# Five exp buffers, nine V buffers, and a reordered end of each group of eight heads in a fused attention and MLP kernel

## The chip, the cores and the metric

The kernel runs on one core of one Trainium2 chip. The metric is the device time of one execution in microseconds (us). The core has a matrix engine (PE, with its weight loads PEld), a vector engine (DVE), an activation engine (ACT), a general engine (POOL) and DMA queues; the queue used here is SyncE's (SP). Each engine runs its own list of instructions in order, and semaphores hold an instruction back until what it needs on another engine is done.

## The reference

Attention over 4 batches and 12 heads, 448 tokens, head size 64, with capped scores, and then a two-layer MLP with the activation h·cos(h). All of it is fp32.

```python
scores = scale * np.matmul(q, k.transpose(0, 1, 3, 2))       # q, k, v: 4 x 12 x 448 x 64
scores = cap * np.tanh(scores / cap)
attn = np.exp(scores - max); attn = attn / (sum(attn) + 1e-09)
x = np.matmul(attn, v)                                       # becomes 1792 x 768
h = x @ w_in                                                 # w_in 768 x 2048
out = (h * np.cos(h)) @ w_out                                # w_out 2048 x 768
```

## The kernel before, in words

**Attention.** The 48 heads are worked through in 6 groups `n` of eight (2 batches by 4 heads). A group has 7 chunks `c` of 64 keys, and a chunk has two score tiles (`a` = 0, 1), so there are 84 score tiles `j` and 42 steps `i`, two tiles to a step. For a step PE makes two score tiles (`scores`, L303, each in one of two PSUM slots of the name `pair`), ACT takes the tanh of each (`tanh`, L321) into one SBUF buffer `t` and the exp of both at once (`exp`, L325). PE then multiplies the exps by V (`values`, L387, halves `e` = 0, 1, summed over the seven chunks in two PSUM buffers `acc`), and DVE adds the exps of six chunks up (`add`, L371, L375). At the end of a group two blocks of matmuls by ones (`sums`, L401) give the denominators in a third `pair` tile `z`: one block reads the last chunk's exps, the other DVE's sum. DVE transposes `z` (`norm_sums`, L412), takes the reciprocal (L419), spreads it (L425), multiplies both `acc` by it into `x0` and `x1` (`norm_scale`, L429), and splits each into a high part (`norm_high`, L434) and a low part (`norm_low`, L437), which are the MLP's input.

**Order.** All of this is called from one list: `at(step, time, call)` gives a call the place 3.4·step + time, the list is sorted, and each engine's instructions stand in that order. The step at whose places a group's denominators are made is called the boundary here (`ends`); it comes when the next group's scores are already under way. Weights are turned from fp64 words to pairs of fp32 parts in between (`Weights`; `DECODE` gives the steps): ACT takes a magnitude (L197), DVE does the rest, the last piece's low part being L230 for the first three pieces.

**Buffers.** A tile of a pool can be written when all readers of the tile that was in its place are done. `t` has 4 buffers, and step 0 uses `x0` and `x1` in place of one. V has 14 places of one chunk. `pair` has two slots in PSUM; `z` takes one of them.

**MLP.** 8 groups of two 128-wide units, 4 blocks of tokens each, 32 steps. For a unit PE makes h (`hidden`, L162), ACT and DVE make h·cos(h) in six operations (`turns` L579, `whole_turns` L582, `reduce` L587 and L588, `cosine` L591, `gate` L594) and split it (`high` L597 on ACT, `low` L600 on DVE); PE multiplies by w_out a step later (L628). Step 0's two units start inside attention: `layers.begin` makes their h in `pair` slots, and `layers.first` takes the first unit up to its gate in the buffer `second`. The MLP's own PSUM tiles (`single`, `rest`) lie where attention's two `acc` were, and its SBUF pools where attention's buffers were.

Of the kernel before, what the change touches and what calls it, by code (L numbers as in the profile page):

```python
# [34 lines left out]
DIRECT = 1  # L35
STEP = 3.4
# [219 lines left out]
class Heads:  # L256


    def __init__(self, ctx, tc, banks, qk, v, capt, inv, xh, xl, bounded):
        nc = tc.nc  # L260
        self.nc, self.qk_in, self.v_in, self.capt, self.inv = nc, qk, v, capt, inv
        if bounded:
            self.inv, self.capt = in_register(nc, inv, "inv"), in_register(nc, capt, "cap")
        self.cap_column = capt
        self.xh, self.xl, self.bounded = xh, xl, bounded
        cp = ctx.enter_context(tc.tile_pool(name="a_const", bufs=1))
        self.ld = ctx.enter_context(tc.tile_pool(name="a_ld", bufs=8 if bounded else 4))
# [8 lines left out]
        self.qk, self.v, self.ps, self.ts, self.half, self.left = {}, {}, {}, {}, {}, {}  # L276
        self.sum, self.acc, self.x, self.z, self.r, self.s = {}, {}, {}, {}, {}, {}
# [34 lines left out]
    def tanh(self, j):  # L312
        i, k = divmod(j, 2)
        if k == 0:
            if i or not self.bounded:
                t = self.ts[i] = self.tp.tile([128, 2, 2, S], F32, name="t", tag="t")
                self.half[i] = [t[:, 0], t[:, 1]]
            else:
                self.half[i] = [self.np.tile([128, 2, S], F32, name=f"x{e}", tag=f"x{e}") for e in range(2)]
            self.left[i] = 2  # L320
        self.nc.scalar.activation(self.half[i][k], self.ps.pop(j)[:, :, 0:S], AF.Tanh, scale=self.inv)  # L321

    def exp(self, i):
        for t in [self.ts[i]] if i else self.half[i]:
            self.nc.scalar.activation(t, t, AF.Exp, scale=self.capt)  # L325

    def t(self, n, a, c):
        j = WHERE[n, a, c]
        return self.half[j // 2][j % 2]

    def used(self, n, c):
        for a in range(2):
            i = WHERE[n, a, c] // 2
            self.left[i] -= 1
            if not self.left[i]:
                self.ts.pop(i, None)
                del self.half[i]
# [115 lines left out]
def attention(ctx, tc, banks, busy, second, qk, v, capt, inv, xh, xl, wts, layers):  # L453
# [24 lines left out]
    for n in range(NO):  # L478
        begin = NC * n
        for c in range(NC):  # L480
            at(begin - 2 * NC + 4 + c if n > 1 else n - 1, 0.3 + 0.1 * c, a.load_v, n, c)
# [3 lines left out]
        for c in range(NC):  # L485
# [8 lines left out]
            if 0 < c < NC - 1:  # L494
                at(i, 0.15, a.add, n, c)
            if c:
                at(i + lag, 0.75 if c == NC - 1 else 2.6 if i == 3 else 0.18, a.used, n, c)
            if c == 1:
                at(i + lag, 2.61 if i == 3 else 0.19, a.used, n, 0)
        for m, (part, args) in enumerate([("sums", ()), ("inverse", ()), ("spread", ()), ("scale", (0,)), ("scale", (1,))]):  # L500
            at(i, 1.0 + 0.1 * m, getattr(a, "norm_" + part), n, *args)
# [14 lines left out]
    at(ND, 1.7, layers.first, second)  # L516
    at(ND + 1, 0.9, layers.begin, 1)
# [130 lines left out]
class Layers:  # L648
    def __init__(self, tc, banks, wts, xh, xl, angles, out):
        self.tc, self.nc, self.banks, self.wts, self.xh, self.xl, self.out = tc, tc.nc, banks, wts, xh, xl, out  # L650
        self.angles, self.half_pi, self.quarter = angles, angles[:, 0:1], angles[:, 1:2]
        self.begun = []
# [13 lines left out]
    def first(self, space):  # L666
# [3 lines left out]
        unit.gone = ("turns", "whole_turns", "reduce", "cosine", "gate")  # L670
        for part in unit.gone:
            getattr(unit, part)()

    def open(self, ctx):
# [13 lines left out]
    def step(self, step, prev, older):  # L688
# [23 lines left out]
        if step == 0:  # L712
            units[1].turns()
            units[1].gone = ("turns",)
# [87 lines left out]
```

## Time and profile before

| what | value |
|---|---|
| median of 3 runs | 630.28 us (629.02 to 630.75) |
| profiled execution | 629.2 us, span 627.4 us |
| PE busy | 612.8 us (98%) |
| DVE busy | 485.7 us (77%) |
| ACT busy | 306.3 us (49%) |
| chain that ended last | PE 90%, ACT 6%, DVE 3% |

The span is what the trace covers of the execution; 1.8 us lie around it. The busy shares are means over two very different stages: attention fills the first quarter, the MLP the rest. The page's slices show PE busy in all, and ACT at 90% or more until the ninth of forty.

### The profile page before, as it was taken

The page shows a single profiled execution, that of the slowest core. Times are in us where ns is not written, and L with a number is a line of the kernel's source. Part 1 is how long each engine was busy: PE and PEld are TensorE (multiplying, and loading weights), DVE is VectorE, ACT ScalarE, POOL GpSimd, SP SyncE. Part 2 cuts the span into 40 slices and gives each one's busy share as a digit, 9 for nine tenths or more (in the row PEclk, how much of TensorE's full clock was granted, in tenths as well). Part 3 has the DMA queues.
Part 4 walks back from the last instruction along what each step waited for, and adds up shares of the span by engine and source line. Part 5 has one row for each costly group of instructions (what it writes and reads, how often), then busy time and mean ns, then how long its engine had stood idle before and what let it go on. Part 6 is the DMA issues. An engine that isn't in the chain of part 4 may idle for free.

```text
span 627.4 us, 11992 instructions
## 1 busy us (share of the span) xinstructions
PE 612.8 (98%) x5206; PEld 472.0 (75%) x5207; DVE 485.7 (77%) x643; ACT 306.3 (49%) x384; POOL 55.3 (9%) x36
## 2 busy tenths in 40 slices
PE   8989999999889999999999999999999999999996
PEld 2333333334779898989989898989899898989895
DVE  1587998886878887888886788888887878887574
ACT  6999999998134343334333333433343333334220
POOL 0000000000111111112011111111111211111000
PEclk9999999999899999999999999999999999999999
DMA  7753445101011111211111111112111111110224
GB/s 222 237 183 122 127 161 165 58 3 52 0 52 50 51 53 52 98 50 52 51 50 51 51 51 51 51 51 86 58 60 50 52 51 50 51 51 1 102 75 182
DMA packets 22783, 48.06 MB, mean 77 GB/s; under 512 B 2497, under 2 KB 9921, under 8 KB 22721
## 3 DMA queue, kind: packets, MB, share of 16 engines
q1 hardware_dynamic: 22576, 47.00, 22.5%
q8 instruction: 43, 0.70, 0.4%
q10 hardware_dynamic: 144, 0.20, 0.1%
q14 instruction: 20, 0.16, 0.1%
HBM read 41.68 MB, written 5.51 MB: 75 GB/s over the span
## 4 chain that ended last, share of the span: by engine, by line
PE 90%; ACT 6%; DVE 3%; issue 0%; DMA 0%; DVEq 0%; ACTq 0%
PE single L162 34%; PE pair L628 25%; PE rest L628 12%; PE pair L303 8%; PE acc L387 7%; ACT t L321 3%; ACT t L325 2%; PE pair L401 1%; PE pair L162 1%; PE idle L63 1%; DVE xl L437 1%; PE acc L63 0%; PE single L628 0%; DVE x L429 0%; DVE gl L600 0%
## 5 line engine op out<-in xcount | busy, mean ns | idle before, releaser
L591 ACT ACTIVATE y<-y,angles 128x384 f32<-128x384 f32 (+1 forms) x63 | 42.3, 672 | 122.9 <-DVE y L588 122.9
L321 ACT ACTIVATE t<-pair 128x896 f32<-128x896 f32 x82 | 72.3, 939 | 4.6 <-PE pair L303 4.5
L387 PE MATMUL acc<-t,v 64*32 64x448 f32 x1312 | 72.9, 536 | 0.0
L303 PE MATMUL pair<-qk 64*32 64x448 f32 x1232 | 70.0, 540 | 2.5 <-ACT t L321 2.0
L325 ACT ACTIVATE t<-t 128x1792 f32<-128x1792 f32 x41 | 70.7, 1728 | 0.0
L641 DVE TENSOR_TENSOR acc<-pair,acc 128x1024 f32<-128x1024 f32 (+1 forms) x56 | 60.8, 1086 | 9.1 <-PE pair L628 8.8
L579 ACT ACTIVATE v<-single,angles 128x384 f32<-128x384 f32 (+1 forms) x62 | 39.2, 632 | 53.0 <-PE single L162 52.8
L597 ACT CAST gh<-y 128x384 fp32r<-128x384 f32 (+1 forms) x63 | 35.8, 569 | 51.1 <-DVE y L594 51.1
L197 ACT ACTIVATE u<-w 128x768 f32<-128x768 f32 x32 | 29.0, 907 | 54.8 <-POOL wo2l L230 10.1
L303 PEld LDWEIGHTS pair<-qk 64*32 64x32 f32 x1232 | 20.8, 106 | 43.9 <-ACT t L321 20.2
L600 DVE TENSOR_TENSOR gl<-y,gh 128x384 fp32r<-128x384 f32 (+1 forms) x63 | 51.9, 823 | 2.5 <-ACT gh L597 2.5
L387 PEld LDWEIGHTS acc<-t,v 64*32 64x32 f32 x1312 | 26.2, 107 | 34.9 <-issue 33.0
L582 DVE TENSOR_SCALAR v<-v 128x384 f32<-128x384 f32 (+1 forms) x63 | 24.5, 388 | 35.2 <-ACT v L579 35.2
L371 DVE TENSOR_TENSOR sum<-sum,t 128x1792 f32<-128x1792 f32 x20 | 40.5, 2025 | 9.8 <-ACT t L325 9.8
L212 DVE TENSOR_SCALAR u<-u 128x768 f32<-128x768 f32 x32 | 17.8, 555 | 32.3 <-ACT u L197 32.2
L588 DVE SCALAR_TENSOR_TENSOR y<-v,y 128x384 f32<-128x384 f32 (+1 forms) x63 | 39.3, 624 | 2.2
L594 DVE TENSOR_TENSOR y<-single,y 128x384 f32<-128x384 f32 (+1 forms) x62 | 38.4, 619 | 3.1 <-ACT y L591 3.1
L587 DVE SCALAR_TENSOR_TENSOR y<-v,single 128x384 f32<-128x384 f32 (+1 forms) x62 | 38.3, 618 | 2.1
L162 PE MATMUL single<-xh,wi0h 128*128 128x384 f32 (+1 forms) x90 | 33.1, 368 | 1.9 <-DVE x L429 1.9
L628 PE MATMUL pair<-gh,wo0l 128*128 128x512 f32 (+1 forms) x96 | 34.9, 363 | 0.0
L628 PE MATMUL pair<-gl,wo0h 128*128 128x512 f32 (+1 forms) x96 | 34.8, 363 | 0.0
L628 PE MATMUL pair<-gh,wo0h 128*128 128x512 f32 (+1 forms) x96 | 34.8, 363 | 0.0
(158 smaller groups left out, 1468.7 us busy)
## 6 DMA issues: line engine op xcount, KB each, us to landing
w<-in_w_in_dram SPq DMA_DIRECT2D x32, 384.0 KB, 3.6
w<-in_w_out_dram SPq DMA_DIRECT2D x32, 384.0 KB, 3.6
qk<-in_qk_dram SPq DMA_DIRECT2D x20, 448.0 KB, 4.4
v<-in_v_dram SPq DMA_DIRECT2D x42, 128.0 KB, 3.5
out_dram<-acc SPq DMA_DIRECT2D x6, 512.0 KB, 2.8
out_dram<-acc SPq DMA_DIRECT2D x5, 384.0 KB, 2.4
qk<-in_qk_dram SPq DMA_DIRECT2D x2, 288.0 KB, 2.9
qk<-in_qk_dram SPq DMA_DIRECT2D x2, 160.0 KB, 3.7
```

The source lines that it names most:

```text
L162: nc.tensor.matmul(h[:, 0:n], lhsT=w[:, ks], rhs=x[:, k, toks], start=(k == 0 and i == 0), stop=(k == KC - 1 and i == 2))
L303: self.nc.tensor.matmul(ps[o:o + 32, h, 0:S], lhsT=x[mine, k:k + 32], rhs=x[mine, Q], start=True, stop=True, tile_position=(64 * h, o))
L321: self.nc.scalar.activation(self.half[i][k], self.ps.pop(j)[:, :, 0:S], AF.Tanh, scale=self.inv)
L325: self.nc.scalar.activation(t, t, AF.Exp, scale=self.capt)
L371: self.nc.vector.tensor_add(out, old, self.ts[NC * n + c])
L387: self.nc.tensor.matmul(self.acc[n, e][o, r], lhsT=self.v[n, c][rows, d], rhs=self.t(n, a, c)[rows, h], start=c == 0, stop=c == NC - 1, ti ...
L579: m.nc.scalar.activation(self.v, self.h, AF.Identity, bias=m.quarter, scale=1.0 / (2.0 * math.pi))
L588: m.nc.vector.scalar_tensor_tensor(self.y, self.v, -TWO_PI_LO, self.y, op0=ALU.mult, op1=ALU.add)
L591: self.m.nc.scalar.activation(self.y, self.y, AF.Sin, bias=self.m.half_pi)
L600: self.m.nc.vector.tensor_sub(self.result(1), self.y, self.result(0))
L628: m.nc.tensor.matmul((y[e] if self.last(i) else y[:, e])[:, 0:n], lhsT=w[:, c], rhs=x[:, j, 0:n], start=(j == 0 and k == 0), stop=(j == GF ...
L641: m.nc.vector.tensor_add(acc, y[:, e, 0:n], acc)
```

## The change

What the diff does, in its parts:

- `t` gets 5 buffers, and step 0 uses one of them like every other step, so its exp is one instruction over both tiles. V gets 9 places; its loads are spread over the steps.
- In the first group the values of chunks 1 to 5 all stand behind the two score tiles of their step (time 2.5).
- At a boundary the two `sums` blocks move from before the boundary's first score tile to between its two score tiles, the second half of the last chunk's values goes behind one further score tile, and the two `norm_scale` follow it.
- In the last group `sums` stands ahead of chunk 5's values. `norm_sums` stands ahead of the first unit's gate, and the previous group's low parts ahead of that unit's work.
- A new `begin_rest` writes out step 0 of the MLP: the two units' operations and the last group's high and low parts are interleaved by hand. The low part of `wo1` goes to DVE (it was on POOL). The weights that the MLP adds get an SBUF pool of their own.

The core of the diff:

```diff
-        self.tp = ctx.enter_context(tc.tile_pool(name="a_t", bufs=4 if bounded else NC))
+        self.tp = ctx.enter_context(tc.tile_pool(name="a_t", bufs=5 if bounded else NC))
-        self.v[n, c] = self.ld.tile([128, 256], F32, name="v", tag="v", bufs=2 * NC if self.bounded else NC)
+        self.v[n, c] = self.ld.tile([128, 256], F32, name="v", tag="v", bufs=NV if self.bounded else NC)
...
-            at(begin - 2 * NC + 4 + c if n > 1 else n - 1, 0.3 + 0.1 * c, a.load_v, n, c)
+            at(max(begin + c - NV + 5, n - 1), 0.3 + 0.1 * c, a.load_v, n, c)
...
+        for c in range(NC - 1):
             i = max(WHERE[n, p, c] for p in range(2)) // 2 + 2
-            lag = 1 if c < NC - 1 and 0 < n and (n, c) not in ((NO - 1, NC - 3), (NO - 1, NC - 2)) else 0
-            if c == NC - 1:
-                at(i, 0.15, a.sums, n, c)
-                at(i, 0.16, a.sums, n, None)
+            step = i + (0 < n and not (last and c == NC - 3))
+            time = (2.5, 2.51) if n == 0 and c else (0.1, 2.0) if n == 0 else (0.17, 0.18) if last and c == NC - 2 else (0.1, 0.1)
             for e in range(2):
-                time = (0.5, 0.7) if c == NC - 1 else (0.1, 2.0) if i == 3 and c == 0 else (2.5, 2.51) if i == 3 else (0.1, 0.1)
-                at(i + lag, time[e], a.values, n, c, e)
+                at(step, time[e], a.values, n, c, e)
...
+        b = begin + NC + 1
+        at(b, 0.15 if last else 0.3, a.sums, n, NC - 1)
+        at(b, 0.16 if last else 0.3, a.sums, n, None)
+        at(b, 0.5, a.values, n, NC - 1, 0)
+        at(b + 1, 1.7, a.values, n, NC - 1, 1)
+        at(b + 1, 1.75, a.used, n, NC - 1)
+        at(b, 1.0, a.norm_sums, n)
+        at(b, 1.1, a.norm_inverse, n)
+        at(b, 1.2, a.norm_spread, n)
         for e in range(2):
-            at(i + 2, 0.5, a.norm_high, n, e)
-            at(i + NC if n < NO - 1 else i + 2, 0.9, a.norm_low, n, e)
+            at(b + 1, 1.8 + 0.1 * e, a.norm_scale, n, e)
+            if not last:
+                at(b + 2, 0.5, a.norm_high, n, e)
+                at(b + NC - (n == NO - 2), 0.9, a.norm_low, n, e)
...
-    at(ND, 1.7, layers.first, second)
-    at(ND + 1, 0.9, layers.begin, 1)
+    at(ND, 1.7, layers.first, second, ("turns", "whole_turns", "reduce", "cosine"))
+    at(ND + 1, 1.05, layers.first, second, ("gate",))
+    at(ND + 2, 1.9, layers.begin, 1)
+    layers.late = [(getattr(a, f"norm_{part}"), NO - 1, e) for part in ("high", "low") for e in range(2)]
...
+    def begin_rest(self):
...
+        first.high()
+        first.low()
+        second.turns()
+        self.wts.high(*self.done)
+        late(0)
+        late(1)
+        second.whole_turns()
+        second.reduce()
+        second.cosine()
+        self.wts.low(*self.done, self.nc.vector)
+        second.gate()
+        second.high()
+        late(2)
+        second.low()
+        late(3)
...
+        wp = ctx.enter_context(self.tc.tile_pool(name="m_w", bufs=1))
         accp = ctx.enter_context(self.tc.tile_pool(name="m_acc", bufs=1))
-        self.wts.open_in(accp, (2, 3))
-        self.wts.open_in(accp, (1, 2), "wo")
+        self.wts.open_in(wp, (2, 3))
+        self.wts.open_in(wp, (1, 2), "wo")
...
         if step == 0:
-            units[1].turns()
-            units[1].gone = ("turns",)
+            self.begin_rest()
+            self.done = piece
+            return cur
```

PE at the boundary of the second group. `qk` rows are score tiles, `t,v` rows values, `t,one` and `sum,one` the two sums; eight matmuls are one block, 16 are two. Before:

```order
L387 MATMUL acc<-t,v 32x448 x16
L401 MATMUL pair<-t,one 32x448 x8
L401 MATMUL pair<-sum,one 32x448 x8
L303 MATMUL pair<-qk 32x448 x8
L387 MATMUL acc<-t,v 32x448 x8
L303 MATMUL pair<-qk 32x448 x8
L387 MATMUL acc<-t,v 32x448 x8
L303 MATMUL pair<-qk 32x448 x16
```

and now:

```order
L382 MATMUL acc<-t,v 32x448 x16
L304 MATMUL pair<-qk 32x448 x8
L396 MATMUL pair<-t,one 32x448 x8
L396 MATMUL pair<-sum,one 32x448 x8
L382 MATMUL acc<-t,v 32x448 x8
L304 MATMUL pair<-qk 32x448 x16
L382 MATMUL acc<-t,v 32x448 x8
L304 MATMUL pair<-qk 32x448 x8
```

One score tile has passed the sums, and one more has passed the second half of the values.

PE where attention ends and the MLP's step 0 begins (`xl,wi0h` is the last of the first unit's 18 matmuls, `xh,wi1h` the first of the second unit's). Before:

```order
L162 MATMUL pair<-xl,wi0h 128x512
L387 MATMUL acc<-t,v 32x448 x16
L401 MATMUL pair<-t,one 32x448 x8
L401 MATMUL pair<-sum,one 32x448 x8
L387 MATMUL acc<-t,v 32x448 x16
L162 MATMUL pair<-xh,wi1h 128x512
```

and now:

```order
L163 MATMUL pair<-xl,wi0h 128x512
L396 MATMUL pair<-t,one 32x448 x8
L396 MATMUL pair<-sum,one 32x448 x8
L382 MATMUL acc<-t,v 32x448 x32
L163 MATMUL pair<-xh,wi1h 128x512
```

The sums have passed two blocks of values; what PE does in all between the two units is the same.

DVE at the same place (`second` and `gl<-second` are the first unit's, `v` and `y` the second unit's; `x_1892` and `x_1894` are the fifth group's, the other `x` the sixth's). Before:

```order
L594 TENSOR_TENSOR second<-pair,second 128x512
L437 TENSOR_TENSOR xl<-x_1892,xh 128x896
L437 TENSOR_TENSOR xl<-x_1894,xh 128x896
L412 STREAM_TRANSPOSE s<-pair 128x896
L419 RECIPROCAL r<-s 128x28
L425 STREAM_TRANSPOSE s<-r 128x896
L429 TENSOR_TENSOR x_2185<-acc,s 128x896
L429 TENSOR_TENSOR x_2187<-acc,s 128x896
L434 CAST xh<-x_2185 128x896
L434 CAST xh<-x_2187 128x896
L437 TENSOR_TENSOR xl<-x_2185,xh 128x896
L437 TENSOR_TENSOR xl<-x_2187,xh 128x896
```

and now:

```order
L407 STREAM_TRANSPOSE s<-pair 128x896
L596 TENSOR_TENSOR second<-pair,second 128x512
L414 RECIPROCAL r<-s 128x28
L420 STREAM_TRANSPOSE s<-r 128x896
L424 TENSOR_TENSOR x_2164<-acc,s 128x896
L424 TENSOR_TENSOR x_2166<-acc,s 128x896
L602 TENSOR_TENSOR gl<-second,gh 128x512
L429 CAST xh<-x_2164 128x896
L429 CAST xh<-x_2166 128x896
L584 TENSOR_SCALAR v<-v 128x512
L589 SCALAR_TENSOR_TENSOR y<-v,pair 128x512
L590 SCALAR_TENSOR_TENSOR y<-v,y 128x512
```

The fifth group's low parts stand ahead of the first unit's work now, the transposition ahead of the gate, and the sixth group's low parts behind the second unit's gate.

## Rows read from the trace of the kernel before

**Rows 1.** Windows: span, then us busy (instructions) of PE, PEld, DVE, ACT, POOL; clock, DMA.
```profile
59.20:82.40 23.20, 22.75 (x496) 9.10 (x486) 20.41 (x18) 22.61 (x22) 0.00 (x0) 1.00 0.48 155
164.40:167.90 3.50, 3.48 (x12) 3.48 (x13) 3.04 (x4) 0.37 (x1) 0.00 (x0) 0.54 0.00 0
183.00:300.00 117.00, 117.00 (x585) 105.34 (x584) 96.25 (x141) 45.01 (x68) 17.23 (x9) 1.00 0.18 61
```

**Rows 2.** Timeline, first group on ACT: start, us, engine, line, operation, [idle before].
```profile
20.50 1.75 ACT L325 ACTIVATE t<-t 128x1792 f32<-128x1792 f32 x1
23.06 1.73 ACT L321 ACTIVATE t<-pair 128x896 f32<-128x896 f32 x2 [0.81 <-PE pair L303]
```

**Rows 3.** Waits between 12 and 149 us: who waited for whom, us, times, longest.
```profile
ACT t L321 <- PE pair L303: 3.8, 11, 0.8
```

**Rows 4.** Timeline of the second group's boundary, PE, ACT and DVE.
```profile
57.65 1.80 ACT L321 ACTIVATE t<-pair 128x896 f32<-128x896 f32 x2
...
58.69 0.99 PE L401 MATMUL pair<-t,one 64*32 64x448 f32 x16
...
59.24 1.79 ACT L325 ACTIVATE t<-t 128x1792 f32<-128x1792 f32 x1
...
60.21 0.96 PE L303 MATMUL pair<-qk 64*32 64x448 f32 x16
...
60.53 1.12 DVE L412 STREAM_TRANSPOSE s<-pair 128x896 f32<-128x896 f32 x1 [1.37 <-PE pair L401]
...
61.28 0.92 ACT L321 ACTIVATE t<-pair 128x896 f32<-128x896 f32 x1 [0.25 <-PE pair L303]
...
63.26 2.09 DVE L429 TENSOR_TENSOR x<-acc,s 128x896 f32<-128x896 f32 x2
...
64.64 0.99 PE L303 MATMUL pair<-qk 64*32 64x448 f32 x16 [0.45 <-ACT t L321]
...
66.92 1.71 PE L303 MATMUL pair<-qk 64*32 64x448 f32 x32
...
68.14 1.72 ACT L321 ACTIVATE t<-pair 128x896 f32<-128x896 f32 x2
```

**Rows 5.** Timeline after the fourth group's boundary: a weight piece's low part, the next magnitude.
```profile
117.61 0.95 DVE L230 TENSOR_TENSOR wo0l<-u,wo0h 128x768 fp32r<-128x768 f32 x1
118.70 0.98 ACT L197 ACTIVATE u<-w 128x768 f32<-128x768 f32 x1
```

**Rows 6.** Timeline from the last sums to the MLP's first products.
```profile
154.28 0.43 DVE L582 TENSOR_SCALAR second<-second 128x512 f32<-128x512 f32 x1 [2.81 <-ACT second L579]
...
156.94 0.69 DVE L594 TENSOR_TENSOR second<-pair,second 128x512 f32<-128x512 f32 x1 [0.79 <-ACT second L591]
...
158.12 0.50 PE L162 MATMUL pair<-xh,wi1h 128*128 128x512 f32 x1
...
162.28 2.09 DVE L429 TENSOR_TENSOR x<-acc,s 128x896 f32<-128x896 f32 x2
...
164.42 0.47 PE L162 MATMUL single<-xh,wi0h 128*128 128x384 f32 x1 [1.93 <-DVE x L429]
...
167.53 0.83 ACT L448 CAST wo1h<-u 128x768 fp32r<-128x768 f32 x1 [4.26 <-DVE xl L437]
...
168.92 1.92 DVE L600 TENSOR_TENSOR gl<-second,gh 128x512 fp32r<-128x512 f32 x1 [1.48 <-ACT gh L597]
170.76 0.42 DVE L582 TENSOR_SCALAR v<-v 128x512 f32<-128x512 f32 x1
...
174.13 0.62 ACT L597 CAST gh<-y 128x512 fp32r<-128x512 f32 x1 [0.76 <-DVE y L594]
...
175.53 0.50 PE L628 MATMUL pair<-gl,wo1h 128*128 128x512 f32 x1
```

**Rows 7.** Chain that ended last, in order of time: start, us, engine and line.
```profile
197.30 6.24 PE single L162 x36
```

**Rows 8.** DMA issues of the page: count, KB each, us from issue to landing.
```profile
v<-in_v_dram SPq DMA_DIRECT2D x42, 128.0 KB, 3.5
```

More of the change, by code (lines that the diff above doesn't have):

```diff
@@ L275, in __init__ @@
             make_identity(nc, self.ident)
-        self.qk, self.v, self.ps, self.ts, self.half, self.left = {}, {}, {}, {}, {}, {}
+        self.qk, self.v, self.ps, self.ts, self.left = {}, {}, {}, {}, {}
         self.sum, self.acc, self.x, self.z, self.r, self.s = {}, {}, {}, {}, {}, {}
@@ L314, in tanh @@
         if k == 0:
[L315 to L319, printed above, removed]
+            self.ts[i] = self.tp.tile([128, 2, 2, S], F32, name="t", tag="t")
             self.left[i] = 2
-        self.nc.scalar.activation(self.half[i][k], self.ps.pop(j)[:, :, 0:S], AF.Tanh, scale=self.inv)
+        self.nc.scalar.activation(self.ts[i][:, k], self.ps.pop(j)[:, :, 0:S], AF.Tanh, scale=self.inv)
     def exp(self, i):
-        for t in [self.ts[i]] if i else self.half[i]:
-            self.nc.scalar.activation(t, t, AF.Exp, scale=self.capt)
+        self.nc.scalar.activation(self.ts[i], self.ts[i], AF.Exp, scale=self.capt)
     def t(self, n, a, c):
         j = WHERE[n, a, c]
-        return self.half[j // 2][j % 2]
+        return self.ts[j // 2][:, j % 2]
     def used(self, n, c):
@@ L335, in used @@
             if not self.left[i]:
-                self.ts.pop(i, None)
-                del self.half[i]
+                del self.ts[i]
     def exp_general(self, n):
@@ L478, in attention @@
     for n in range(NO):
-        begin = NC * n
+        begin, last = NC * n, n == NO - 1
         for c in range(NC):
-            at(begin - 2 * NC + 4 + c if n > 1 else n - 1, 0.3 + 0.1 * c, a.load_v, n, c)
+            at(max(begin + c - NV + 5, n - 1), 0.3 + 0.1 * c, a.load_v, n, c)
         for p in range(4):
@@ L484, in attention @@
                 at(begin - NC + (-1, 2, 3, 4)[p] if n > 1 else -0.5, 0.8, a.load, n, p // 2, p % 2)
-        for c in range(NC):
+        for c in range(NC - 1):
             i = max(WHERE[n, p, c] for p in range(2)) // 2 + 2
-            lag = 1 if c < NC - 1 and 0 < n and (n, c) not in ((NO - 1, NC - 3), (NO - 1, NC - 2)) else 0
-            if c == NC - 1:
-                at(i, 0.15, a.sums, n, c)
-                at(i, 0.16, a.sums, n, None)
+            step = i + (0 < n and not (last and c == NC - 3))
+            time = (2.5, 2.51) if n == 0 and c else (0.1, 2.0) if n == 0 else (0.17, 0.18) if last and c == NC - 2 else (0.1, 0.1)
             for e in range(2):
-                time = (0.5, 0.7) if c == NC - 1 else (0.1, 2.0) if i == 3 and c == 0 else (2.5, 2.51) if i == 3 else (0.1, 0.1)
-                at(i + lag, time[e], a.values, n, c, e)
-            if 0 < c < NC - 1:
+                at(step, time[e], a.values, n, c, e)
+            if c:
                 at(i, 0.15, a.add, n, c)
-            if c:
-                at(i + lag, 0.75 if c == NC - 1 else 2.6 if i == 3 else 0.18, a.used, n, c)
+                at(step, time[1] + 0.05, a.used, n, c)
             if c == 1:
-                at(i + lag, 2.61 if i == 3 else 0.19, a.used, n, 0)
-        for m, (part, args) in enumerate([("sums", ()), ("inverse", ()), ("spread", ()), ("scale", (0,)), ("scale", (1,))]):
-            at(i, 1.0 + 0.1 * m, getattr(a, "norm_" + part), n, *args)
+                at(step, time[1] + 0.06, a.used, n, 0)
+        b = begin + NC + 1
[7 more added lines that the diff above has]
+        at(b, 1.2, a.norm_spread, n)
         for e in range(2):
-            at(i + 2, 0.5, a.norm_high, n, e)
-            at(i + NC if n < NO - 1 else i + 2, 0.9, a.norm_low, n, e)
+            at(b + 1, 1.8 + 0.1 * e, a.norm_scale, n, e)
+            if not last:
+                at(b + 2, 0.5, a.norm_high, n, e)
+                at(b + NC - (n == NO - 2), 0.9, a.norm_low, n, e)
     pieces = (("wi", 0), ("wi", 1), ("wo", 0), ("wo", 1), ("wi", 2))
@@ L651, in __init__ @@
         self.angles, self.half_pi, self.quarter = angles, angles[:, 0:1], angles[:, 1:2]
-        self.begun = []
+        self.begun, self.late = [], []
         self.todo = [None]
@@ L664, in sine, with first, late @@
         self.nc.scalar.activation(self.angles[:, 2:3], self.angles[:, 1:2], AF.Sin)
-    def first(self, space):
+    def first(self, space, parts):
         unit = self.begun[0]
         unit.space = {"v": space[:, 0:WIDE], "y": space[:, WIDE:2 * WIDE]}
-        unit.gone = ("turns", "whole_turns", "reduce", "cosine", "gate")
-        for part in unit.gone:
+        for part in parts:
             getattr(unit, part)()
+        unit.gone += parts
+    def begin_rest(self):
+        def late(k):
+            if self.late:
+                call, *args = self.late[k]
+                call(*args)
+        first, second = self.begun
+        for part in ("turns", "whole_turns", "reduce", "cosine", "gate"):
+            if part not in first.gone:
+                getattr(first, part)()
+        first.high()
[13 more added lines that the diff above has]
+        late(3)
     def open(self, ctx):
```

1 line of the change is left out of this document (added).

## The prediction

> **What bounds the kernel now.** I read the windows first. Past 183 us PE is busy in 117.00 of 117.00 us [rows 1]: the MLP runs at PE's own pace there, and the change does not touch its work. Whatever is gained or lost arises before, and arrives at the end as a shift. Between two boundaries of attention, PE is busy 22.75, ACT 22.61 and DVE 20.41 of 23.20 us [rows 1]: three engines nearly full, so a wait that is taken away on one comes up soon on another. Next I read the waits of that stage: ACT stood 3.8 us, 11 times, for score tiles [rows 3]. Last the timeline of the handover: PE stood 1.93 us for `norm_scale`, came back at a clock of 0.54 for 3.50 us, and then waited for the second unit's high part, which DVE and ACT had not made [rows 1, 6]. These are three places, and the change touches all three.
>
> **First group.** The exp that begins at 20.50 is followed by a tanh at 23.06 [rows 2]. An exp keeps ACT for 1.59 us when nothing is waited for; so do two tanhs (57.65 to 59.24) [rows 4]. The tanh could have begun at 22.09; 0.97 us are lost, since four blocks of values (chunks 1 and 2) stand on PE ahead of its score tile. The change puts chunk 2 behind the next step's score tiles, and PE, with a block every 0.75 us (two blocks of sums between 58.69 and 60.21 [rows 4]), makes them before 22.09. **-0.97 us.** The single exp in step 0 replaces two over half the width; the same elements pass through ACT, so I take nothing, between -0.2 and +0.2.
>
> **A boundary.** In the second group ACT begins an exp at 59.24 and could go on at 60.83; the tanh comes at 61.28, 0.45 us late [rows 4]. Its score tile (60.21) stands behind the sums, and the sums wait until 58.69 for the PSUM slot that the tanh from 57.65 frees. Now the score tile takes that slot at 58.69, is there by 59.8, and the tanh is on time. Five boundaries with 0.45 us make 2.3 us, if nothing else were late.
>
> Something else is late. The sums stand one block later, at 59.45 in place of 58.69, and with them the transposition (60.53 to 61.29) and `norm_scale` (63.26 to 64.0): 2.73 us lie between those two, as now. The first scale ends at 65.05 and the second at 66.05. Behind these stand the next group's first values, which need both `acc`. The score tile that begins at 64.64 follows a tanh that is 0.45 us earlier, so it begins at 64.19, and its block is done at 64.95. Half e=0 then waits until 65.1, half e=1 until 66.1, and the next score tile comes at 66.87: now it is 66.92. So PE gains 0.05 us, and its tanh, 1.07 us behind its score tile, comes at 67.95 in place of 68.14. Of 0.45 us a boundary keeps 0.05 on PE and 0.2 on ACT.
>
> The delay of 0.75 us on DVE costs more at the fourth group. There DVE's low part ends at 118.56 and the magnitude that overwrites its input begins on ACT at 118.70 [rows 5]. With the chain from the transposition on 0.75 us later, the low part ends at 119.3, and ACT, which could go on at 118.5, waits 0.8 us: this boundary ends 0.6 us worse than now. I add -0.2 for three boundaries, +0.6 for the fourth, and -0.05 for the last, since from there on PE runs without a wait into the MLP: about -0.1 in all, between -2.3 (each keeps its 0.45) and +3.0 (each goes as the fourth). Attention together: **-1.1 us**, and the trace of before shows no case nearer to the new order than these.
>
> **V in nine places, five exps.** A load now stands until the values of nine chunks before are done, and is issued some seven steps, over 20 us, before its own values. A load lands 3.5 us after its issue [rows 8]. The queue on SP holds the next group's q and k behind these loads, also steps ahead of their use. I take nothing; below it is a rival. The five exps give DVE and PE one more step to release a buffer; no row shows ACT waiting for one, so this too is nothing.
>
> **The handover.** I follow it with the times of before, without attention's shift. PE ends the second unit's 18 matmuls at 162.49, from where it stands 1.93 us; it would begin the next 36 at 164.42 [rows 6]. Those 36 take 6.24 us at full clock (one such run later [rows 7]), so a matmul of 512 columns takes 6.24/36·4/3 = 0.23 us. Without any wait the third product with the second unit, which is at 175.53 now [rows 6], would come at 162.49 + 6.24 + 5·0.23 = 169.88: 5.65 us earlier. The question is whether DVE and ACT are ready.
>
> - *acc.* The fifth group's low parts (2.1 us) go into DVE's idle 2.81 us ahead of 154.28. The sums are two blocks (1.5 us) earlier. DVE comes to the transposition at 156.15 (156.94 less the idle 0.79); the sums are done by 155.3 (158.12 less six blocks, plus two and 0.3 for the last to end). `norm_scale` begins 2.73 us and one gate (0.69) later at the most, at 159.6, and ends at 161.7. PE asks for that at 162.49: no wait, 0.8 us of slack.
> - *First gate.* It now stands behind the transposition (1.11) and runs from 157.3 to 158.0 in place of 156.94. The second unit's matmuls need its PSUM slot; they begin at 158.12 now. Slack 0.1 us; if it is gone, PE loses as much, up to 0.3.
> - *Second unit.* Its high part of `wo1` waits 4.26 us on ACT for the last low part now, and the first unit's halves stand behind it until 170.8. In the new order neither stands there. After `norm_scale` DVE has one low part (0.69) and two casts (1.1) to do, to 163.5. From there to the second unit's high part it takes 4.0 us now (170.76 to 174.75 [rows 6]), and the low part of `wo1`, which DVE takes over from POOL, adds 0.95 (as the one at 117.61 [rows 5]) less the cosine that it lies beside: 167.7. PE needs it at 169.4. The low part follows one of attention's (1.05) and is there at 168.9; PE needs it at 169.88, 1.0 us of slack.
>
> So **-5.65 us**, if the clock stays up. The row says 0.54 of full speed for 3.50 us, close to the lower level of 1.2 GHz, right after the 1.93 us in which PE did nothing [rows 1, 6]. This stretch costs 3.50·(1-0.54) = 1.6 us. The Trainium skill (TensorE: Matmul & The Clock Gate, What's actually happening) says that the lower clock is the state that the engine rests in and that activity is what lifts it; by that, PE without the idle place keeps 2.4 GHz, and the sum stays -5.65. If the fall had another cause, such as the small tiled matmuls before it, the sum would be -4.05; no run here shows that case yet.
>
> **Sum.** 629.2 - 1.1 - 5.65 = 622.4 us against the profiled execution. The median of the three runs is 1.1 us above it, their spread 1.7 us; set against the median the sum is 623.5. I predict 623.0.
>
> **The rivals.**
> 1. *The boundaries keep everything.* DVE has more room than I think, and each keeps its 0.45 us: 623.0 - 2.2 = 620.8. For it: DVE is the least full of the three. Against: the second scale cannot end before the sums that it divides by.
> 2. *The clock falls all the same*, or the first gate holds PE: 623.0 + 1.6 = 624.6. For it: the slack of 0.1 us at the gate. Against: the row before the fall is an idle one.
> 3. *DVE is the bound at each boundary*: all five go as the fourth, 623.0 + 3.1 = 626.1. For it: PE, ACT and DVE are all near full. Against: at the other boundaries no magnitude stands right behind a low part.
> 4. *The handover is not opened*: a new wait on an old buffer takes the place of the one on `wo1`, and only the first idle place goes: about 623.0 + 3.7 = 626.7. Against: the new pool lies over buffers whose readers are on PE and were done long before.
> 5. *V comes too late.* Nine places are two more than a group. If the queue holds a load until less than 3.5 us are left, values stand on PE, ACT follows. Each group would stand up to 3.5 us, five groups 17 us: 640, slower than before. It decides from 1.5 us a group on (7.3 us / 5). Against: over 20 us between issue and use.
>
> **How the numbers follow.** Forecast 0.60, rival 1 0.13, rival 2 0.13, rival 3 0.06, rival 4 0.05, rival 5 0.03. A measurement of this kernel can tell 0.3% (1.9 us) from no change. All cases but the last are over 2 us faster; I leave 0.02 for a mix of 3 and 4 that comes out even. Faster 0.95, same 0.02, slower 0.03. The range takes in rivals 1 to 3 and the uneven spread of the runs: 620.3 to 626.3.
>
> **What would show it.** Right: at 162 us PE goes from the second unit to the next step's matmuls without a gap and at a clock of 1.00; the products wait for nothing; the tanh after a boundary's exp comes without idle time, while the first values of the next group wait for `norm_scale`, and the magnitude after the fourth boundary waits some 0.8 us for DVE; the first group's idle 0.81 us is gone. Wrong: a clock below 1.00 after attention, values that wait for a DMA, or a PE that waits at the second unit for the first gate by more than 0.3 us.

## The result, and the profile after

| what | before | after |
|---|---|---|
| median | 630.51 us (4 runs, 629.02 to 631.31) | 623.38 us (4 runs, 622.50 to 623.74) |
| profiled execution, span | 629.2, 627.4 us | 623.17, 621.3 us |
| PE, DVE, ACT busy | 612.8, 485.7, 306.3 us | 611.9, 484.1, 305.7 us |
| chain that ended last | PE 90%, ACT 6%, DVE 3% | PE 93%, DVE 3%, ACT 2% |

The ratio is 0.9888, with a 95% interval of 0.9866 to 0.9909: faster by 1.1%. 623.0 us were forecast. The busy times hardly differ; what went is idle time of PE and the stretch at the lower clock.

The windows of the kernel after, for the stretches that answer to [rows 1] (span, then us busy of PE, PEld, DVE, ACT, POOL, clock, DMA):

```profile
58.15:81.35 23.20, 23.19 (x489) 8.88 (x480) 20.26 (x18) 22.69 (x23) 0.00 (x0) 1.00 0.47 150
161.65:167.92 6.27, 6.27 (x38) 6.27 (x37) 5.88 (x9) 4.04 (x6) 0.00 (x0) 1.00 0.00 0
176.50:293.50 117.00, 117.00 (x585) 105.33 (x584) 95.95 (x141) 44.80 (x68) 17.24 (x9) 1.00 0.18 59
```

Between two boundaries PE is busy in 23.19 of 23.20 us (22.75 before), yet the stretch is as long as it was: part of what the profile counts as busy is waiting, as in the values at 64.17 further down, which take 1.98 us where four blocks take 1.71 elsewhere. The second row is the first 36 matmuls behind attention, at a clock of 1.00 where it was 0.54. The MLP is as full as before.

**The handover.** The chain that ended last, kernel after, from the first unit's matmuls to the first products (start, us, engine and line):

```profile
148.38 4.30 PE pair L163 x18
152.68 1.67 PE pair L396 x32
154.34 3.01 PE acc L382 x64
157.35 4.30 PE pair L163 x18
161.65 6.26 PE single L163 x36
167.92 5.48 PE pair L630 x24
```

Each row ends where the next begins: PE waits for nothing from 148.38 to 173.40. What made the room is on DVE and ACT. Their timeline in the kernel after:

```profile
155.23 1.11 DVE L407 STREAM_TRANSPOSE s<-pair 128x896 f32<-128x896 f32 x1
156.26 0.65 DVE L596 TENSOR_TENSOR second<-pair,second 128x512 f32<-128x512 f32 x1
...
158.40 2.09 DVE L424 TENSOR_TENSOR x<-acc,s 128x896 f32<-128x896 f32 x2
160.40 0.68 DVE L602 TENSOR_TENSOR gl<-second,gh 128x512 fp32r<-128x512 f32 x1
...
162.34 0.82 ACT L443 CAST wo1h<-u 128x768 fp32r<-128x768 f32 x1
162.47 0.43 DVE L584 TENSOR_SCALAR v<-v 128x512 f32<-128x512 f32 x1 [0.32 <-ACT v L581]
...
166.75 0.69 DVE L602 TENSOR_TENSOR gl<-y,gh 128x512 fp32r<-128x512 f32 x1
```

The scales end at 160.49, 1.2 us before PE asks for them (161.65). The first gate ends at 156.91, 0.4 us before the second unit's matmuls. The high part of `wo1` no longer waits 4.26 us [rows 6], the first `gl` takes 0.68 us where it took 1.92 [rows 6], and the second unit's `gl` is there at 167.44. The third product with the second unit begins at 168.91 (175.53 before [rows 6]).

**Attention.** The first group on ACT, kernel after, answering to [rows 2]:

```profile
20.33 1.74 ACT L321 ACTIVATE t<-t 128x1792 f32<-128x1792 f32 x1
21.91 1.77 ACT L318 ACTIVATE t<-pair 128x896 f32<-128x896 f32 x2
```

The idle 0.81 us is gone. The second group's boundary, kernel after, answering to [rows 4]:

```profile
59.78 1.01 ACT L318 ACTIVATE t<-pair 128x896 f32<-128x896 f32 x1
...
63.02 2.09 DVE L424 TENSOR_TENSOR x<-acc,s 128x896 f32<-128x896 f32 x2
...
64.17 1.98 PE L382 MATMUL acc<-t,v 64*32 64x448 f32 x32
64.32 0.92 ACT L318 ACTIVATE t<-pair 128x896 f32<-128x896 f32 x1 [0.33 <-PE pair L304]
...
65.94 1.71 PE L304 MATMUL pair<-qk 64*32 64x448 f32 x32
...
67.00 1.73 ACT L318 ACTIVATE t<-pair 128x896 f32<-128x896 f32 x2 [0.17 <-PE pair L304]
```

The tanh behind the boundary's exp (59.78) waits for nothing now. But the values at 64.17 take 1.98 us for four blocks, which take 1.71 elsewhere, since they wait for the scales; the score tiles behind them come at 65.94, and the tanh at 67.00 has a wait that it did not have. At the first boundary that wait is 0.37 us. At the third there is none: ACT takes a weight's magnitude in that place, and the tanh comes behind it anyway (the rows at 89.91 and 90.77):

```profile
43.02 1.73 ACT L318 ACTIVATE t<-pair 128x896 f32<-128x896 f32 x2 [0.37 <-PE pair L304]
...
89.91 0.95 ACT L198 ACTIVATE u<-w 128x768 f32<-128x768 f32 x1
90.77 1.72 ACT L318 ACTIVATE t<-pair 128x896 f32<-128x896 f32 x2
```

Behind the fourth boundary the timeline of the kernel after answers to [rows 5]:

```profile
116.86 0.95 DVE L231 TENSOR_TENSOR wo0l<-u,wo0h 128x768 fp32r<-128x768 f32 x1
...
117.84 0.96 ACT L198 ACTIVATE u<-w 128x768 f32<-128x768 f32 x1 [0.63 <-DVE wo0l L231]
```

That wait is new too. All of it in one view, the waits of the kernel after from 12 to 149 us (who waited for whom, us, times, longest):

```profile
PEld acc L382 <- DVE x L424: 8.1, 10, 0.9
...
ACT t L318 <- PE pair L304: 2.9, 9, 0.4
...
PEld acc L382 <- DMA v<-in_v_dram: 0.2, 1, 0.2
```

ACT's wait for score tiles fell from 3.8 us [rows 3] to 2.9 us, nearly all of it the first group's 0.81. The only wait for a V load is one of 0.2 us.

### The profile page after: what moved, and what is told of

It reads as the page before. It is cut to its first block, busy times and chain, and to the rows that moved or that the text cites. A ratio compares the mean times of both kernels' runs of the same rounds, so it can differ in the third digit from the quotient of the medians.

```text
span 621.3 us, 11987 instructions
## 1 busy us (share of the span) xinstructions
PE 611.9 (98%) x5207; PEld 468.9 (75%) x5207; DVE 484.1 (78%) x644; ACT 305.7 (49%) x383; POOL 53.5 (9%) x35
## 4 chain that ended last, share of the span: by engine, by line
PE 93%; DVE 3%; ACT 2%; DMA 1%; issue 0%; SPq 0%; DVEq 0%; ACTq 0%
PE single L163 36%; PE pair L630 25%; PE rest L630 12%; PE pair L304 8%; PE acc L382 8%; PE pair L396 2%; PE pair L163 1%; DMA v<-in_v_dram 1%; ACT t L318 1%; DVE x L424 1%; DVE sum L366 1%; PE idle L64 1%; DVE s L407 1%; DVE s L420 1%; ACT u L198 0%; PE acc L64 0%
## 5 line engine op out<-in xcount | busy, mean ns | idle before, releaser
L318 ACT ACTIVATE t<-pair 128x896 f32<-128x896 f32 x84 | 74.8, 958 | 6.4 <-PE pair L304 6.4
L382 PE MATMUL acc<-t,v 64*32 64x448 f32 x1344 | 74.2, 537 | 0.2
L321 ACT ACTIVATE t<-t 128x1792 f32<-128x1792 f32 x42 | 73.0, 1741 | 0.0
L304 PE MATMUL pair<-qk 64*32 64x448 f32 x1232 | 68.6, 541 | 2.0 <-ACT t L318 2.0
L584 DVE TENSOR_SCALAR v<-v 128x384 f32<-128x384 f32 (+1 forms) x63 | 24.3, 386 | 36.1 <-ACT v L581 36.1
L590 DVE SCALAR_TENSOR_TENSOR y<-v,y 128x384 f32<-128x384 f32 (+1 forms) x63 | 39.3, 624 | 2.2
L163 PE MATMUL single<-xl,wi2h 128*128 128x512 f32 (+1 forms) x96 | 34.7, 362 | 0.0
```

What stands on the lines that cost most here:

```text
L163: nc.tensor.matmul(h[:, 0:n], lhsT=w[:, ks], rhs=x[:, k, toks], start=(k == 0 and i == 0), stop=(k == KC - 1 and i == 2))
L304: self.nc.tensor.matmul(ps[o:o + 32, h, 0:S], lhsT=x[mine, k:k + 32], rhs=x[mine, Q], start=True, stop=True, tile_position=(64 * h, o))
L318: self.nc.scalar.activation(self.ts[i][:, k], self.ps.pop(j)[:, :, 0:S], AF.Tanh, scale=self.inv)
L321: self.nc.scalar.activation(self.ts[i], self.ts[i], AF.Exp, scale=self.capt)
L382: self.nc.tensor.matmul(self.acc[n, e][o, r], lhsT=self.v[n, c][rows, d], rhs=self.t(n, a, c)[rows, h], start=c == 0, stop=c == NC - 1, ti ...
L590: m.nc.vector.scalar_tensor_tensor(self.y, self.v, -TWO_PI_LO, self.y, op0=ALU.mult, op1=ALU.add)
```

## The experiments

The kernel before was run beside each batch: 631.29 us (13 runs, 629.01 to 632.93) beside attention_only, old_boundary, gate_first and split_values, 631.15 beside double_idle, late_unit, pool_low and low_early, 631.26 beside four_exps and gate_first_again. Ratios are against it. Traces begin up to 0.7 us apart; where two traces of attention are compared here, it is from the second exp of the first group (13.96 us after, 14.13 before) to the first unit's matmuls (148.38 and 149.19): 134.42 us after, 135.06 before.

**attention_only.** The new attention with the old handover.

```diff
...
+            at(b + (2 if last else NC), 0.9, a.norm_low, n, e)
...
-    layers.late = [(getattr(a, f"norm_{part}"), NO - 1, e) for part in ("high", "low") for e in range(2)]
...
-        wp = ctx.enter_context(self.tc.tile_pool(name="m_w", bufs=1))
...
-            self.begin_rest()
...
+            units[1].turns()
+            units[1].gone = ("turns",)
...
```

> The changed attention (five exps, nine V, first group, boundaries) with the handover of before (order of the sixth group's end, first unit's gate ahead of the transposition, one pool for the added weights and the accumulator, low part of wo1 on POOL). Theory (the handover is worth 5.7 us by itself, attention 0.8): 629.7 us, some 6 us above the changed kernel; PE stands 1.9 us ahead of step 1's first matmul, then runs at about half clock for 3.5 us, and waits for the second unit's high part. Rival (attention carries the gain and the handover is hidden behind something later): at most 626.

630.68 us (10 runs, 628.71 to 632.01), ratio 0.9986 (0.9968 to 1.0005): 7.3 us above the kernel after, where some 6 were expected. Nearly the whole gain is the handover; by this ratio alone, attention's part can't be told from nothing, while in the trace attention takes 134.37 us, 0.69 less than before. The timeline has the old waits, PE 1.93 us for the scale and 1.60 us for the second unit:

```profile
163.63 0.44 PE L163 MATMUL single<-xh,wi0h 128*128 128x384 f32 x1 [1.93 <-DVE x L424]
...
166.74 0.83 ACT L443 CAST wo1h<-u 128x768 fp32r<-128x768 f32 x1 [4.26 <-DVE xl L432]
...
174.01 0.50 PE L628 MATMUL pair<-gh,wo1h 128*128 128x512 f32 x1 [1.60 <-ACT gh L597]
```

The windows show what was not expected: the clock falls behind the second idle place too, which it does not do in the profile of the kernel before.

```profile
173.00:174.00 1.00, 0.00 (x0) 0.00 (x0) 0.32 (x2) 0.66 (x2) 0.00 (x0) 1.00 0.00 0
...
175.00:176.00 1.00, 1.00 (x4) 0.82 (x4) 0.96 (x3) 0.23 (x1) 0.00 (x0) 0.66 0.00 0
176.00:177.00 1.00, 1.00 (x4) 0.71 (x4) 0.93 (x3) 0.00 (x0) 0.00 (x0) 0.50 0.00 0
```

Each of its two falls costs 1.6 us: the 36 matmuls from 163.63 on take 7.91 us, 6.26 in the kernel after, and 19 products from 174.73 on take 6.05, 4.46 in the kernel before. Two idle places of 1.93 and 1.60 us and two falls make 6.8 of the 7.3 us.

**old_boundary.** The kernel after with the sums ahead of the boundary's first score tile again.

```diff
-        at(b, 0.15 if last else 0.3, a.sums, n, NC - 1)
+        at(b, 0.15, a.sums, n, NC - 1)
...
-        at(b + 1, 1.7, a.values, n, NC - 1, 1)
+        at(*((b + 1, 1.7) if last else (b, 0.7)), a.values, n, NC - 1, 1)
...
-            at(b + 1, 1.8 + 0.1 * e, a.norm_scale, n, e)
+            at(*((b + 1, 1.8 + 0.1 * e) if last else (b, 1.3 + 0.1 * e)), a.norm_scale, n, e)
```

> The changed kernel with the boundary order of before (sums ahead of both score tiles, norm_scale right behind them), all else as changed. Theory (what the tanh gains at a boundary, the first values of the next group give back, and the fourth boundary loses 0.6 us): within 0.5 us of the changed kernel, 623.4; each boundary's first tanh waits again (0.25 to 0.35 us idle), the magnitude after the fourth no longer waits, and the first values of a group don't wait for norm_scale. Rival (each boundary keeps its 0.45 us): 2.2 us slower, 625.6.

622.83 us (4 runs), ratio 0.9881 (0.9852 to 0.9911). Attention takes 134.12 us, 0.30 less than after. In its timeline the tanh's wait is back and the magnitude's is gone:

```profile
60.40 0.92 ACT L318 ACTIVATE t<-pair 128x896 f32<-128x896 f32 x1 [0.25 <-PE pair L304]
...
117.81 0.96 ACT L198 ACTIVATE u<-w 128x768 f32<-128x768 f32 x1
```

The reordered boundary is worth nothing here; by the two traces it costs 0.3 us, which the times of four runs each can't tell from nothing.

**gate_first**, and **gate_first_again** for more executions of the same kernel. The first gate stands ahead of the transposition, chunk 5's values ahead of the sums, and the fifth group's low parts where they were.

```diff
-            time = (2.5, 2.51) if n == 0 and c else (0.1, 2.0) if n == 0 else (0.17, 0.18) if last and c == NC - 2 else (0.1, 0.1)
+            time = (2.5, 2.51) if n == 0 and c else (0.1, 2.0) if n == 0 else (0.1, 0.11) if last and c == NC - 2 else (0.1, 0.1)
...
-                at(b + NC - (n == NO - 2), 0.9, a.norm_low, n, e)
+                at(b + NC, 0.9, a.norm_low, n, e)
...
-    at(ND + 1, 1.05, layers.first, second, ("gate",))
+    at(ND, 1.75, layers.first, second, ("gate",))
```

> The changed kernel with three places undone: the sixth group's sums behind chunk 5's values, the first unit's gate ahead of the transposition, the fifth group's low parts between the two. Theory (an idle PE lets the clock fall): PE stands about 2 us ahead of step 1's first matmul, the clock then is about 0.54 for 3.5 us, together 3.6 us: 627.0. Rival (the fall has another cause than the idle place): only the 2 us, 625.4, with a clock of 1.00 behind it. Second rival (DVE hides it): 623.4.

> The kernel with the gate ahead of the transposition once more, for more executions of its idle place of 1.9 us, since with 4.0 us (double_idle) the clock fell and with 1.9 us it did not in four executions. Theory A (1.9 us of idle PE can bring the low clock, as in most executions of the kernel before, by chance): some executions near 626.5 to 627 us at a mean clock of 0.994 or less, the others at 625.2. Rival B (1.9 us are too short, and the fall in the kernel before needs its second idle place too): all executions between 624.7 and 625.6 us at a clock of 0.997 or more.

625.17 us (4 runs), ratio 0.9916 (0.9886 to 0.9946), then 625.16 (6 runs), ratio 0.9912 (0.9892 to 0.9933). PE stands 1.93 us as in the kernel before, and the kernel loses 1.8 us, not the 3.6 of the first theory: the rival is met. Its windows in the first of the two runs, the idle place and the 36 matmuls behind it:

```profile
161.83:163.76 1.93, 0.01 (x2) 0.00 (x1) 1.93 (x3) 1.41 (x2) 0.00 (x0) 1.00 0.00 0
163.76:170.11 6.35, 6.35 (x36) 6.35 (x37) 6.28 (x10) 2.15 (x4) 0.00 (x0) 1.00 0.00 0
```

The clock stays at 1.00, in the profile of the second run too. Of the ten executions one took 626.76 us at a mean clock of 0.995, the other nine 624.79 to 625.75 at 0.997 or more. That one is 1.6 us above the median, the price of one fall in attention_only, so a fall seems to follow this idle place too, but seldom. That is theory A of the second run, which had expected 0.994 or less; no profile shows it.

**double_idle.** gate_first with the fifth group's low parts computed twice, so that DVE comes later and PE stands 4.18 us.

```diff
...
                 at(b + NC, 0.9, a.norm_low, n, e)
+                if n == NO - 2:
+                    at(b + NC, 0.9, a.norm_low, n, e)
...
```

> The kernel with the gate ahead of the transposition (gate_first), but the fifth group's two low parts are computed twice: PE's idle place ahead of the MLP's step 1 grows by 2.1 us, from 1.9 to 4.0 us. Its wait grows by the same, and nothing else is changed. Theory A (an idle place costs only its own length, and the low clock after it in the kernel before came from something else): clock 1.00 from there on, 625.2 + 2.1 = 627.3 us, small spread between runs. Rival B (an idle place of PE brings the low clock, and 1.9 us is only too short): a clock near 0.5 for some 3 us after it, 629 us, or runs in two groups at 627.3 and 629.

629.53 us (10 runs, 628.85 to 630.27), ratio 0.9980 (0.9967 to 0.9992): 4.4 us more than gate_first for 2.25 us more idle. The windows:

```profile
161.70:164.53 2.83, 0.01 (x1) 0.00 (x0) 2.66 (x4) 1.41 (x2) 0.00 (x0) 1.00 0.00 0
164.53:165.88 1.35, 0.00 (x0) 0.00 (x0) 1.35 (x3) 0.00 (x0) 0.00 (x0) 0.50 0.00 0
165.88:171.36 5.48, 5.48 (x17) 5.48 (x18) 5.41 (x9) 1.28 (x3) 0.00 (x0) 0.50 0.00 0
```

The clock falls to 0.50 (1.2 GHz) while PE stands, 2.83 us after its last matmul, and stays there for the first 5.48 us of work: 17 matmuls in place of some 32. An idle PE does bring the lower clock: behind 1.93 us it came in some executions and not in others, at 4.18 us the profile shows it, and no execution was near the 627.3 us of a held clock.

**late_unit.** Step 0 with the last group's low parts ahead of the second unit again, `wo1`'s low part on POOL, the pool of its own kept.

```diff
         second.turns()
-        self.wts.high(*self.done)
         late(0)
         late(1)
+        late(2)
+        late(3)
+        self.wts.high(*self.done)
...
-        self.wts.low(*self.done, self.nc.vector)
+        self.wts.low(*self.done)
...
```

> The kernel after, but in step 0 of the MLP the last group's casts and low parts all stand ahead of the high part of wo1 and of the second unit's work on DVE, and wo1's low part is POOL's again; the pool of its own for the weights stays. Theory A (the gain at the second unit is the pool of its own, which lets the high part of wo1 begin without waiting for attention's last low parts; the interleaved order has a slack of about 1 us to spare): two low parts (2.1 us) come ahead of the gate, one of which stood ahead of the second unit's low part anyway, so that part comes 1.05 us later against about 1 us of slack, and the high part 2.1 later against about 1.7: 0 to +1, best 623.9 us. Rival B (the order is what opens it): as the second idle place of the kernel before, +3.7, 627.1 us. PE at the second unit's 18 matmuls and at the next 36 unchanged in both.

624.60 us (4 runs), ratio 0.9903 (0.9885 to 0.9921): 1.2 us more than after, a little past theory A's bound and far from B's 3.7. The timeline:

```profile
162.20 2.09 DVE L432 TENSOR_TENSOR xl<-x,xh 128x896 fp32r<-128x896 f32 x2
...
162.46 0.83 ACT L443 CAST wo1h<-u 128x768 fp32r<-128x768 f32 x1
...
163.37 2.62 POOL L231 TENSOR_TENSOR wo1l<-u,wo1h 128x768 fp32r<-128x768 f32 x1 [158.53 <-ACT wo1h L443]
...
164.20 2.07 DVE L584 TENSOR_SCALAR v<-v 128x512 f32<-128x512 f32 x1
...
169.91 0.50 PE L630 MATMUL pair<-gh,wo1h 128*128 128x512 f32 x1 [1.17 <-ACT gh L599]
```

The high part of `wo1` runs beside the low parts that it waited 4.26 us for in attention_only: the pool of its own releases it. What the estimate lacked is the row at 164.20, where an operation of 0.43 us took 2.07 beside POOL's. These 1.64 us are more than PE's wait of 1.17; by that, an estimate, the order alone costs little. No run has the pool of its own with the order of before and nothing else, or this order without POOL's operation.

**pool_low.** After, with only `wo1`'s low part on POOL.

```diff
-        self.wts.low(*self.done, self.nc.vector)
+        self.wts.low(*self.done)
```

> The kernel after with one edit: the low part of wo1 in step 0 is POOL's, as in the kernel before, in place of DVE's. Theory A (slack hides it): DVE is rid of 0.95 us there; operations that stand beside POOL's 1.84 us may take 1.9 in place of 0.7 us; the second unit's parts come up to 1 us later or earlier, PE waits for neither: 623.4 us, within 0.5. Rival B (the move away from POOL is part of the gain): the second unit's low part misses its time by 0.5 to 1 us: 624.1 us.

623.39 us (4 runs), ratio 0.9884 (0.9866 to 0.9901), as after (623.38). Its timeline shows the price and that the slack hides it:

```profile
163.43 1.86 POOL L231 TENSOR_TENSOR wo1l<-u,wo1h 128x768 fp32r<-128x768 f32 x1 [158.62 <-ACT wo1h L443]
...
163.85 1.98 DVE L590 SCALAR_TENSOR_TENSOR y<-v,y 128x512 f32<-128x512 f32 x1
```

**four_exps.** After, with four exp buffers.

```diff
-        self.tp = ctx.enter_context(tc.tile_pool(name="a_t", bufs=5 if bounded else NC))
+        self.tp = ctx.enter_context(tc.tile_pool(name="a_t", bufs=4 if bounded else NC))
```

> The kernel after with four buffers for the exps in place of five; the order is the same. Theory A (the prediction's: no wait for a buffer is taken away by the fifth, it is worth nothing): 623.4 us. Rival B (the fifth buffer is what the later values of the first group need: with the values of chunks 1 to 5 behind their step's score tiles an exp buffer is held longer, and with four buffers a tanh of the first group waits some 1.9 us for PE's values; from then on PE and ACT carry the shift): a tanh near 20 us with an idle of about 1.9 us, all later work 2.0 us later, 625.4 us.

624.95 us (4 runs), ratio 0.9907 (0.9881 to 0.9933), and attention takes 136.39 us, 1.97 more than after. The timeline names the wait, a tanh that may not write where PE still reads exps:

```profile
20.90 1.73 ACT L318 ACTIVATE t<-pair 128x896 f32<-128x896 f32 x2 [1.72 <-PE acc L382]
```

**low_early.** After, with the third weight piece's low part one step earlier.

```diff
-DECODE = [(8, 8, 8, 8, 11, 12), (13, 14, 18, 19, 20, 21), (25, 25, 26, 27, 28, 32), (33, 35, 39, 40)]
+DECODE = [(8, 8, 8, 8, 11, 12), (13, 14, 18, 19, 20, 21), (25, 25, 26, 27, 28, 31), (33, 35, 39, 40)]
```

> The kernel after with one edit: the low part of the third weight piece is made one step earlier, ahead of the fourth boundary's scales. Theory A: the magnitude behind the fourth boundary no longer waits (0.63 us idle now), all that follows comes 0.7 us earlier: 622.7 us, and the first values of the groups still wait for the scale as in the kernel after. Rival B (the gain of 2.2 us with split values came from this edit alone): 621.2 us. Rival C (the low part now delays the transposition or the scale itself): 623.4 us.

This was run after split_values, to tell its two edits apart. 622.53 us (4 runs), ratio 0.9869 (0.9852 to 0.9886); attention 133.63 us, 0.79 less than after. The magnitude waits for nothing:

```profile
117.73 0.95 ACT L198 ACTIVATE u<-w 128x768 f32<-128x768 f32 x1
```

In the kernel after it begins at 117.84, though there the second exp of the first group came 0.66 us earlier (13.96 against 14.62). Theory A's size is met.

**split_values.** low_early, and the next group's first values apart: each half between two score tiles, where the two scales are ready.

```diff
+            if n and c == 0:
+                time = 1.7, 2.5
```

> The changed kernel with the next group's first values split around its two score tiles (half e=0 behind the first, half e=1 behind the second), so that no score tile stands behind a wait for norm_scale, and the third weight piece's low part one step earlier, ahead of the magnitude that waits for it. Theory (these two are what the boundaries lost): attention ends 1.9 us earlier, 621.5; no wait of the magnitude, and the tanh two steps after a boundary without idle time. Rival (DVE is the bound at a boundary, so the wait only moves): 623.4.

621.18 us (4 runs, 620.71 to 621.87), ratio 0.9855 (0.9825 to 0.9885): the best version, 2.2 us faster than after. Attention takes 132.44 us, 1.98 less. Behind the second boundary, in its timeline:

```profile
64.19 0.92 ACT L318 ACTIVATE t<-pair 128x896 f32<-128x896 f32 x1 [0.34 <-PE pair L304]
...
66.59 1.71 ACT L318 ACTIVATE t<-pair 128x896 f32<-128x896 f32 x2
```

The last tanh comes without the 0.17 us: here a boundary keeps most of what the reordered sums free. From the second boundary on, the stretch to the next one (to the first unit's matmuls for the last) is 0.36 to 0.41 us shorter than in the kernel before, against the 0.45 of rival 1; the first is 0.12 shorter. Less low_early's 0.79, the split alone is worth 1.19 us over five boundaries.

## Why the prediction was right, point by point

- **First group.** -0.97 was forecast. From the exp at 20.33 to the tanh is 1.58 us now, 2.56 before: -0.98. Right.
- **Five exps: nothing.** Wrong as a statement on the part alone. ACT waited for no buffer in the trace of before, but the same change holds the first group's exps longer. four_exps shows what would have come: 1.72 us of idle. The fifth buffer is the price of the first group's gain, and the sum came out right since both were made together.
- **A boundary.** The mechanism is the forecast one: the first tanh is on time, and the first values wait for the scale (8.1 us, 10 times, in the table of waits). All five sizes are within 0.3 us of the forecast. The stretch from one boundary to the next (to the first unit's matmuls for the last) changed by +0.07, -0.06, -0.44, +0.70 and +0.04 us, against -0.2, -0.2, -0.2, +0.6 and -0.05. Their sum is +0.31 where -0.05, put as about -0.1, was forecast. The working had the pair of tanhs behind the late values late too, but by too little, and left 0.2 us of the gain; at the second boundary 0.06 were left, at the first and the fifth nothing. It also took the third as the others, where a magnitude of ACT's fills the place of the wait (89.91) and the whole gain stays. Rival 1, in which each boundary keeps its 0.45, held at the third alone; rival 3, in which each goes as the fourth, at the fourth alone.
- **The fourth boundary.** Right: the magnitude waited 0.63 us for DVE's low part (0.8 forecast), and low_early gave 0.79 us back when that was taken away.
- **Attention in all.** -1.1 forecast; the first unit's matmuls came 0.81 us earlier, 0.64 of it inside attention and the rest from the start of the trace. The term was 0.3 to 0.5 too good, and that lies at the boundaries.
- **V.** Right: one wait of 0.2 us.
- **The handover.** -5.65 forecast. The third product with the second unit moved by 168.91 - 175.53 = -6.62, less attention's -0.81: -5.81. Each readiness was early by more than forecast: the scale 1.2 us (0.8), the gate 0.4 (0.1), the low part 1.5 (1.0). The 155.3 at which the sums were to be done adds up to 155.4, which changes nothing. The idle places alone don't make the sum: gate_first brings back the first and loses 1.8 us, late_unit 1.17 us of the second and loses 1.2, attention_only both and loses 7.3, of which two falls of the clock are 3.2.
- **The clock.** 1.6 us of the handover's term stood on the claim that the clock falls because PE stands. The runs bear it out, but not as surely as the text had it. The idle 1.93 us is followed by 0.54 in the profile of before and by 0.50 in attention_only, here 1.43 us after the work had begun again:

```profile
161.70:163.63 1.93, 0.01 (x1) 0.00 (x0) 1.93 (x3) 0.69 (x1) 0.00 (x0) 1.00 0.00 0
163.63:165.06 1.43, 1.43 (x8) 1.43 (x9) 1.43 (x3) 0.00 (x0) 0.00 (x0) 1.00 0.00 0
165.06:168.50 3.44, 3.44 (x13) 3.44 (x12) 1.97 (x3) 1.35 (x2) 0.85 (x1) 0.50 0.00 0
```

  These are the windows of attention_only. The same idle place in gate_first has no fall in its two profiles, and 4.18 us have one. Of the second idle place, 1.61 us in before and 1.60 in attention_only, only the latter has one behind it (0.50 from 176 to 177 us). The rule that the Trainium skill gives (TensorE: Matmul & The Clock Gate, What's actually happening), that the throttled clock is the resting state and activity lifts it, agrees with double_idle: 0.50 after 2.83 us without a matmul. At the end of each trace, where PE has nothing left to do, the clock falls as well: 2.6 us after the last matmul in low_early (615.28 to 617.88), 5.0 in old_boundary (615.31 to 620.27). The other cause that the prediction named, the small tiled matmuls, is not borne out: they stand ahead of the same place in the kernel after, and its clock is 1.00. So a short idle place doesn't always bring the fall; the term was right because the profile that it was worked out from has one. Why the fall behind 1.93 us is in both profiles of the kernels with two idle places and in neither of gate_first stays open.
- **The sum.** Against the profiled execution 622.4 was forecast and 623.17 came (+0.3 attention, -0.2 handover; the trace ends, with the output's transfer, 5.31 us after the last compute where it was 4.66 before, +0.65). Against the median 623.5 stands beside 623.38. Part of that is luck. The profiled execution of before, with one fall, was one of its faster ones, and the 1.1 us that its median stands above it were carried over to the kernel after, whose profile has no fall at all. Over its executions beside the first batch (13) it ranged over 3.9 us with mean clocks from 0.992 to 1.000, the kernel after (4) over 1.2 us with 0.997 to 1.000; it seems, and is not shown for single executions, that the falls went with the idle places.

## What to carry to other kernels

Where one stage hands over to the next, look at where the tiles of the new stage lie: a cast that stood 4.26 us behind the old stage's last readers was free once it had memory of its own, while its place in the order, with POOL's operation beside it, cost 1.2 us. A wait moved off one engine in a stretch where three are nearly full comes up again a few instructions later, so put the consumer where its input is ready (the split values) before moving the producer. A buffer count that no wait in the old trace asks for can still be what a new order needs.

## What the runs showed of the hardware

- The fall of the clock came 2.83 us (double_idle) and 3.36 us (attention_only, 161.70 to 165.06) after the last matmul ahead of the idle place, in the second case into work that had run at 1.00 for 1.43 us. The lower clock so hits matmuls that don't follow the idle place directly, and 1.93 us of idle PE could cost 1.6 us more than their length.
- DVE operations beside a two-input POOL operation took 1.98 us for 0.69 (L590 in pool_low, two inputs in SBUF) and 2.07 for 0.43 (L584 in late_unit, one input). POOL's own took 2.62 us in late_unit, where it began beside a two-input DVE operation (until 164.29), and 1.86 in pool_low. The Trainium skill (SBUF — State Buffer, SBUF: two separate sides) has it that the two engines share one pair of ports, which whichever of certain DVE operations and a POOL operation starts first holds to its end. The rows agree: the slow DVE operations end 0.3 us (166.27 and 165.99, late_unit) and 0.5 us (165.83 and 165.29, pool_low) after POOL's.
